# Block-sparse attention with an attention mixture of experts: pairs of heads of the next batch placed between the stages of this one, and one score matmul per query block

## The chip, the cores and the metric

The kernel runs on one core of a Trainium2 chip. The metric is device microseconds (us) for one execution, lower is better. Before the change it took 298.99 us, the median of three runs (298.35 to 299.44).

In what follows, PE is the matrix engine (TensorE; PEld is its loading of weights), DVE the vector engine, ACT the scalar engine, POOL GpSimd, and SP the engine that issues most DMAs. L123 means line 123 of the kernel as it is printed below.

## The reference: what is computed

There are 4 batches, 8 heads, 768 tokens and 64 elements per head. Two layers follow one another.

Layer one is a sparse attention. A query sees the keys at a distance under 16 tokens, and besides them 24 summaries, one for each block of 32 tokens: the summary's key is the elementwise maximum over the block, its value the mean, and log(32) is added to its score. One softmax goes over both kinds.

```
scores_l = where(|i - j| < 16, scale * q @ k.T, -1e9)
scores_s = scale * q @ k_sum.T + log(32)
x = softmax([scores_l, scores_s]) @ [v, v_sum]
```

Layer two takes the heads side by side as x (768 x 512 per batch). A gate picks two of four experts per token with softmaxed weights. Each expert is a causal attention with 64-element queries, keys and values of its own and an output projection back to 512; the output is the weighted sum over the two chosen experts.

## The kernel before

The Tile framework takes the program in the order in which it is written, gives out the buffers and the semaphores, and may move an instruction ahead of others on its engine when its own estimate says that the engine would wait. Each engine then takes its instructions strictly in the order so built; only weight loads of PE run ahead. PSUM (eight banks) is given out from two groups: "one" (one bank, four buffers) and "two" (two banks, two buffers).

The main loop at the end (L336) runs, for each batch, all of `stage1` and then all of `stage2`. Where the next batch's work is independent, the build moves a few of its instructions ahead, no more.

**stage1** (L114) first makes the sums of v by blocks of 32: POOL adds halves of a 96 x 2048 tile, five adds each (L123). Then it goes over four pairs of heads (L128):
- POOL issues the loads of q and k, converting them to 16 bits on the way (L133); 128 consecutive tokens lie across the partitions, six such tiles.
- SP issues the loads of v into `v_blk`, 96 keys on the partitions for each of 12 blocks of 64 queries (L142, L145), and of the block sums into rows 96 to 119 (L148).
- PE transposes q and k (L153, L158), DVE evicts them (L155, L160) and takes the maxima of k over blocks (L162).
- For each head PE writes the mask into the scores by a matmul with the identity (L171), adds the local scores, twelve matmuls of 96 keys by 64 queries with 64 rows contracted (L178), and adds the summaries' scores (L184). Each block's window of 96 keys begins 16 tokens ahead of its queries, but is clamped at both ends (`win_start`).
- ACT takes the exp (L188). PE multiplies with the values in fp32 (L196); column 64 of `v_blk` is a constant and gives the softmax's denominator. DVE divides (L200, L201), PE transposes x (L206), and ACT and DVE split it into two 16-bit parts, hi and lo (L209, L210).

**stage2** (L215) has four parts. *Values and gate*: PE computes the values of the four experts and the gate's logits (L224, L227), DVE copies them (L231, L233) and runs the gate, a dozen operations on 24 elements (L247 to L259). *Two expert parts* (cc = 0 and 1, two experts each): q and k projections (L268), evicted by DVE (L273) and ACT (L275); scores by groups of key tiles (L288), the exp on ACT (L293), the causal cut of the diagonal blocks on POOL (L298), the values (L307), the division and the gate's weight on DVE (L310 to L313), and a transpose (L317, L319). *Output*: the projection (L325), evicted by ACT and DVE (L329, L331), stored by SP (L332).

The weights of stage 2 are loaded after stage 1 of batch 0 is issued (`load_stage2_weights`, L83), through POOL's queue.

Of the kernel before, what the change touches and what calls it, by code (L numbers as in the profile page):

```python
# [8 lines left out]
FP32 = mybir.dt.float32  # L9
# [5 lines left out]
B = 4  # L15
H = 8
S = 768
# [20 lines left out]
def win_start(t):  # L38
    return min(max(64 * t - 16, 0), S - WIN)


@with_exitstack
def kernel(
# [13 lines left out]


# [3 lines left out]
    make_identity(nc, ident32)  # L62

    maskb = consts.tile((128, NQ, 64), HALF, name="maskb")
    nc.gpsimd.memset(maskb, 0.0)
    for t0, t1 in ((0, 1), (1, NQ - 1), (NQ - 1, NQ)):
        shift = 64 * t0 - win_start(t0)
        m = maskb[0:WIN, t0:t1, :]
        n = t1 - t0

        nc.gpsimd.affine_select(m, m, [[0, n], [-1, 64]], AL.is_ge, NEG,
                                base=15 - shift, channel_multiplier=1)
        nc.gpsimd.affine_select(m, m, [[0, n], [1, 64]], AL.is_ge, NEG,
                                base=15 + shift, channel_multiplier=-1)
# [8 lines left out]
    def load_stage2_weights():  # L83
        nc.sync.dma_start(out=wg_f32,
                          in_=moe_w_gate.rearrange("(c p) g -> p c g", p=128))
        for e in range(E):
            cc, ep = divmod(e, 2)
            for j, wsrc in enumerate((moe_wq, moe_wk)):
                nc.gpsimd.dma_start(out=wqk[:, :, cc, j, 64 * ep:64 * ep + 64],
                                    in_=wsrc[e].rearrange("(c p) d -> p c d", p=128))  # L90
            nc.gpsimd.dma_start(out=wvg[:, :, 64 * e:64 * e + 64],
                                in_=moe_wv[e].rearrange("(c p) d -> p c d", p=128))
        for cc in range(2):
            nc.gpsimd.dma_start(out=wo_cat[cc],
                                in_=moe_wo[2 * cc:2 * cc + 2].rearrange("e d n -> (e d) n"))
        nc.vector.tensor_copy(wvg[:, :, 256:260], wg_f32)
        nc.vector.tensor_copy(wg_hi32, wvg[:, :, 256:260])
        nc.vector.tensor_tensor(wg_lo32, wg_f32, wg_hi32, AL.subtract)
        nc.vector.tensor_scalar(wvg[:, :, 260:264], wg_lo32, LO_SCALE, None, AL.mult)


    NVB = 4
    v_bufs = [consts.tile((128, 2, NQ, 65), FP32, name=f"v_blk{i}") for i in range(NVB)]
    for i in range(NVB):
        nc.gpsimd.memset(v_bufs[i][:, :, :, 64:65], 1.0 / XS)
        nc.gpsimd.memset(v_bufs[i][96:128, :, :, 64:65], 32.0 / XS)


    NV2 = 2
    v2_bufs = [consts.tile((128, NT, E, 65), HALF, name=f"v2_{i}") for i in range(NV2)]  # L110
    for i in range(NV2):
        nc.gpsimd.memset(v2_bufs[i][:, :, :, 64:65], XS)

    def stage1(b):  # L114
        xT_hi, xT_lo = [], []
        vsums = []
        for g in range(2):
            v_s = s1.tile((96, 2048), FP32, name="v_s", bufs=2)
            nc.sync.dma_start(out=v_s,
                              in_=v[b, 4 * g:4 * g + 4].rearrange("h (n s) d -> (h n) (s d)", s=32))  # L120
            half = 1024
            while half >= 64:
                nc.gpsimd.tensor_tensor(v_s[:, 0:half], v_s[:, 0:half],  # L123
                                        v_s[:, half:2 * half], AL.add)
                half //= 2
            vsums.append(v_s)

        for c in range(NCH):  # L128
            q_nat = s1.tile((128, NT, 128), HALF, name="q_nat", bufs=3)
            k_nat = s1.tile((128, NT, 128), HALF, name="k_nat", bufs=3)  # L130
            for src, dst in ((q, q_nat), (k, k_nat)):
                for hp in range(2):
                    nc.gpsimd.dma_start(  # L133
                        out=dst[:, :, 64 * hp:64 * hp + 64],
                        in_=src[b, 2 * c + hp].rearrange("(t p) d -> p t d", p=128))
            v_blk = v_bufs[(NCH * b + c) % NVB]
            vb = v[b, 2 * c:2 * c + 2]
            for hp in range(2):
                vh = v[b, 2 * c + hp]
                src = bass.AP(vh.tensor, vh.offset + 48 * D,  # L140
                              [[D, WIN], [64 * D, NQ - 2], [1, D]])
                nc.sync.dma_start(out=v_blk[0:WIN, hp, 1:NQ - 1, 0:64], in_=src)  # L142
                src = bass.AP(vh.tensor, vh.offset,
                              [[D, WIN], [(S - WIN) * D, 2], [1, D]])
                nc.sync.dma_start(out=v_blk[0:WIN, hp, 0:NQ:NQ - 1, 0:64], in_=src)  # L145
                hh = 2 * (c % 2) + hp
                vs = vsums[c // 2][NSUM * hh:NSUM * hh + NSUM, 0:64]
                nc.sync.dma_start(out=v_blk[WIN:KR, hp, :, 0:64],  # L148
                                  in_=vs.unsqueeze(1).to_broadcast((NSUM, NQ, 64)))

            qT_ps = ps.tile((128, NT, 128), HALF, name="qT_ps", tag="one", bufs=4)
            for t in range(NT):
                nc.tensor.transpose(qT_ps[:, t, :], q_nat[:, t, :], ident16)  # L153
            qT = s1.tile((128, S), HALF, name="qT", bufs=2)
            nc.vector.tensor_copy(qT, qT_ps.rearrange("p t n -> p (t n)"))  # L155
            kT_ps = ps.tile((128, NT, 128), HALF, name="kT_ps", tag="one", bufs=4)
            for t in range(NT):
                nc.tensor.transpose(kT_ps[:, t, :], k_nat[:, t, :], ident16)  # L158
            kT = s1.tile((128, S), HALF, name="kT", bufs=2)
            nc.vector.tensor_copy(kT, kT_ps.rearrange("p t n -> p (t n)"))  # L160
            ksum = s1.tile((128, NSUM), HALF, name="ksum", bufs=2)
            nc.vector.tensor_reduce(ksum, kT.rearrange("p (n w) -> p n w", w=32),  # L162
                                    AX.X, AL.max)

            aTs = []
            sps = []
            for hp in range(2):
                sc = ps.tile((128, 1024), FP32, name="sc", tag="two", bufs=2)
                sps.append(sc)
                for lo, hi in ((0, 512), (512, 768)):  # L170
                    nc.tensor.matmul(sc[:, lo:hi], ident16,  # L171
                                     maskb.rearrange("p t n -> p (t n)")[:, lo:hi],
                                     start=True, stop=False, skip_group_check=True)
            for t in range(NQ):
                for hp in range(2):
                    rows = slice(64 * hp, 64 * hp + 64)
                    w0 = win_start(t)
                    nc.tensor.matmul(sps[hp][0:WIN, 64 * t:64 * t + 64],  # L178
                                     kT[rows, w0:w0 + WIN], qT[rows, 64 * t:64 * t + 64],
                                     start=False, stop=False, skip_group_check=True)  # L180
            for hp in range(2):
                rows = slice(64 * hp, 64 * hp + 64)
                for lo, hi in ((0, 512), (512, 768)):
                    nc.tensor.matmul(sps[hp][WIN:KR, lo:hi], ksum[rows, :], qT[rows, lo:hi],  # L184
                                     start=False, stop=True, skip_group_check=True)
            for hp in range(2):
                aT = s1.tile((128, S), FP32, name="aT", bufs=4)
                nc.scalar.activation(aT[0:KR, :], sps[hp][0:KR, 0:S], AF.Exp, scale=SCALE)  # L188
                aTs.append(aT)

            x32 = s1.tile((128, NT, 128), FP32, name="x32", bufs=2)
            for hp in range(2):
                av = ps.tile((128, NT, 65), FP32, name="av", tag="one", bufs=4)
                for t in range(NQ):
                    o = 64 * (t % 2)
                    nc.tensor.matmul(av[o:o + 64, t // 2, :],  # L196
                                     aTs[hp][0:KR, 64 * t:64 * t + 64],
                                     v_blk[0:KR, hp, t, :], start=True, stop=True)
                rec = s1.tile((128, NT, 1), FP32, name="rec", bufs=4)
                nc.vector.reciprocal(rec, av[:, :, 64:65])  # L200
                nc.vector.tensor_tensor(x32[:, :, 64 * hp:64 * hp + 64], av[:, :, 0:64],  # L201
                                        rec.to_broadcast((128, NT, 64)), AL.mult)
# [168 lines left out]
```

The softmax here doesn't subtract the row's maximum and nothing guards it: scores larger than these inputs give would overflow.

## Time and profile before

One execution was profiled. Its time and what it shows in sum:

| | |
|---|---|
| median of the three runs | 298.99 us |
| the profiled execution, its own time | 300.52 us |
| its span, first to last instruction | 298.8 us |
| mean granted TensorE clock | 0.859 of full |
| PE busy / DVE / ACT / POOL | 218.1 / 123.0 / 96.0 / 127.1 us |
| DMA | 32.10 MB in 109001 packets, 104880 of them under 512 bytes |
| POOL's issues of q and k loads (L133) | 64, 53.6 us together |
| PE matmul instructions | 2448 |

The columns of a timeline row are: start and length in us, engine, line, operation, out<-in, how many; in brackets how long the engine had been idle before it and what released it. A row of a table by stretch has the stretch, its length, the busy time of PE, PEld, DVE, ACT and POOL with the number of instructions in parentheses, the granted clock, the share of the DMA engines and GB/s. In the page's slices each digit is the busy share of a fortieth of the span in tenths; for PEclk it is the granted clock.

Busy time says little by itself here: an engine that waits for another half of the time shows as half busy, and the end is set by the chain through several of them.

### The profile page before, as it was taken

Reading aid. Unit: us, or ns where it says so; the run is one execution under the profiler, and the core shown is the slowest. Engines: PE = TensorE matmul, PEld = TensorE weight load, DVE = VectorE, ACT = ScalarE, POOL = GpSimd, SP = SyncE. Lnnn points to the kernel's source line nnn. Section 1 sums busy time; section 2 is a strip of 40 time slices with the busy share of each in tenths; the row PEclk is TensorE's granted clock in tenths of the full one; section 3 lists DMA queues with packets and bytes.
Section 4 is the critical chain, followed back from the end, with each engine's and each line's share of the span. In section 5 each row is a group of like instructions: output and inputs, shape, how many; then the busy total and the mean of one; then the engine's idle time right before and its main releaser. Section 6 shows DMA issues by size and latency. Waiting matters only on the chain.

```text
span 298.8 us, 5906 instructions
## 1 busy us (share of the span) xinstructions
PE 218.1 (73%) x2448; PEld 140.8 (47%) x2448; DVE 123.0 (41%) x280; ACT 96.0 (32%) x117; POOL 127.1 (43%) x191
## 2 busy tenths in 40 slices
PE   1004998492678798877978888697789799679683
PEld 0002766360245466653544666462555566545340
DVE  0002655348042456654407366361425555461231
ACT  1001233205325433316261333307242433225612
POOL 7998543599603444892134249903024000003110
PEclk9999999867587999998675999976867999895957
DMA  7899999993920999939205999993009300000005
GB/s 199 124 81 173 169 168 191 135 119 50 176 49 0 155 232 220 171 79 177 56 0 39 309 225 103 157 184 70 2 0 133 133 2 2 2 0 2 0 0 211
DMA packets 109001, 32.10 MB, mean 107 GB/s; under 512 B 104880, under 2 KB 105136, under 8 KB 108208
## 3 DMA queue, kind: packets, MB, share of 16 engines
q0 software_dynamic: 56800, 7.35, 38.5%
q1 hardware_dynamic: 52176, 24.39, 37.7%
q8 instruction: 19, 0.31, 0.4%
q14 instruction: 6, 0.05, 0.1%
HBM read 30.42 MB, written 6.29 MB: 123 GB/s over the span
## 4 chain that ended last, share of the span: by engine, by line
PE 46%; DVE 22%; ACT 12%; POOL 9%; DMA 5%; issue 4%; SPq 0%; ACTq 0%; POOLq 0%
PE sp L288 7%; PE pp L268 6%; POOL v_s L123 6%; PE av L196 6%; PE av L307 6%; DVE xT_lo L210 5%; ACT a L293 4%; PE op L325 4%; PE sc L178 4%; ACT aT L188 4%; DVE ksum L162 4%; DVE x L201 4%; PE vp L224 3%; PE sc L171 3%; DMA v_s<-in_v_dram 3%
## 5 line engine op out<-in xcount | busy, mean ns | idle before, releaser
L298 POOL TENSOR_SCALAR_AFFINE_SELECT a<-a 128x256 f16<-128x256 f16 x48 | 19.4, 406 | 102.5 <-ACT a L293 102.5
L293 ACT ACTIVATE a<-sp 128x1024 f16<-128x1024 f32 (+1 forms) x48 | 41.2, 921 | 13.4 <-PE sp L288 13.4
L188 ACT ACTIVATE aT<-sc 120x768 f32<-120x768 f32 x32 | 25.5, 810 | 54.3 <-PE sc L184 54.3
L133 POOL DMA_DIRECT2D q_nat<-in_q_dram x32 | 26.9, 850 | 36.8 <-PE qT_ps L153 31.6
L123 POOL TENSOR_TENSOR v_s<-v_s 96x1024 f32<-96x1024 f32 (+4 forms) x40 | 40.6, 1023 | 3.4 <-DMA v_s<-in_v_dram 1.8
L288 PE MATMUL sp<-qkT,qkT 64*128 64x512 f16 (+3 forms) x128 | 27.8, 364 | 19.0 <-ACT a L293 10.4
L196 PE MATMUL av<-v_blk,aT 120*64 120x65 f32 x768 | 29.8, 231 | 5.1 <-ACT aT L188 2.9
L196 PEld LDWEIGHTS av<-v_blk,aT 120*64 120x64 f32 x768 | 25.9, 143 | 12.4 <-ACT aT L188 7.0
L307 PEld LDWEIGHTS <-a 128*128 128x128 f16 x336 | 20.3, 129 | 21.1 <-POOL a L298 17.8
L307 PE MATMUL av<-v,a 128*128 128x65 f16 x336 | 25.5, 242 | 5.1 <-POOL a L298 5.0
L209 ACT CAST xT_hi<-xT_ps 128x768 f16<-128x768 f32 x16 | 12.8, 798 | 47.4 <-PE xT_ps L206 47.4
L310 DVE RECIPROCAL r<-av 128x6 f32<-128x6 f32 x16 | 3.0, 190 | 60.6 <-PE av L307 60.6
L133 POOL DMA_DIRECT2D k_nat<-in_k_dram x32 | 26.7, 854 | 1.5 <-DMA k_nat<-in_k_dram 1.5
L200 DVE RECIPROCAL rec<-av 128x6 f32<-128x6 f32 x32 | 6.3, 196 | 50.5 <-PE av L196 50.5
L268 PE MATMUL pp<-xT_hi,wqk 128*128 128x512 f16 (+1 forms) x128 | 27.0, 358 | 0.0
L178 PEld LDWEIGHTS <-kT 64*96 64x96 f16 x384 | 18.8, 126 | 10.4 <-issue 5.7
L171 PE MATMUL sc<-maskb,ident 128*128 128x512 f16 x64 | 16.1, 337 | 10.3 <-DVE xT_lo L210 5.0
L178 PE MATMUL sc<-qT,kT 64*96 64x64 f16 x384 | 22.3, 212 | 0.6 <-DVE kT L160 0.6
L224 PE MATMUL vp<-wvg,xT_hi 128*128 128x264 f16 x96 | 19.1, 342 | 4.8 <-DMA wvg<-in_moe_wv_dram 3.1
L288 PEld LDWEIGHTS <-qkT 64*128 64x128 f16 x128 | 8.8, 98 | 28.0 <-issue 12.0
L153 PE MATMUL qT_ps<-ident,q_nat 128*128 128x128 f16 x96 | 9.4, 244 | 15.7 <-DMA q_nat<-in_q_dram 15.7
L325 PE MATMUL op<-wo_cat,wT 128*128 128x512 f16 x48 | 19.1, 536 | 1.1 <-DVE wT L319 0.7
(62 smaller groups left out, 272.1 us busy)
## 6 DMA issues: line engine op xcount, KB each, us to landing
v_blk<-in_v_dram SPq DMA_DIRECT2D x32, 240.0 KB
v_s<-in_v_dram SPq DMA_DIRECT2D x8, 768.0 KB
out_dram<-o_sb SPq DMA_DIRECT2D x12, 512.0 KB
q_nat<-in_q_dram POOLq DMA_DIRECT2D x32, 96.0 KB, 5.3
k_nat<-in_k_dram POOLq DMA_DIRECT2D x32, 96.0 KB, 6.5
v_blk<-v_s SPq DMA_DIRECT2D x32, 72.0 KB
v_blk<-in_v_dram SPq DMA_DIRECT2D x32, 48.0 KB
wqk<-in_moe_wq_dram POOLq DMA_DIRECT2D x4, 64.0 KB, 13.3
```

The lines of the kernel that those rows point to most:

```text
L123: nc.gpsimd.tensor_tensor(v_s[:, 0:half], v_s[:, 0:half], v_s[:, half:2 * half], AL.add)
L133: nc.gpsimd.dma_start(out=dst[:, :, 64 * hp:64 * hp + 64], in_=src[b, 2 * c + hp].rearrange("(t p) d -> p t d", p=128))
L171: nc.tensor.matmul(sc[:, lo:hi], ident16, maskb.rearrange("p t n -> p (t n)")[:, lo:hi], start=True, stop=False, skip_group_check=True)
L178: nc.tensor.matmul(sps[hp][0:WIN, 64 * t:64 * t + 64], kT[rows, w0:w0 + WIN], qT[rows, 64 * t:64 * t + 64], start=False, stop=False, skip_ ...
L188: nc.scalar.activation(aT[0:KR, :], sps[hp][0:KR, 0:S], AF.Exp, scale=SCALE)
L196: nc.tensor.matmul(av[o:o + 64, t // 2, :], aTs[hp][0:KR, 64 * t:64 * t + 64], v_blk[0:KR, hp, t, :], start=True, stop=True)
L224: nc.tensor.matmul(vp[:, i, 0:264], xT_hi[ch][:, cols], wvg[:, ch, :], start=(ch == 0), stop=False, skip_group_check=True)
L268: nc.tensor.matmul(pp[:, lo:hi], wqk[:, ch, cc, j, :], xT_hi[ch][:, lo:hi], start=(ch == 0), stop=(ch == NCH - 1))
L288: nc.tensor.matmul(sp[:, c0:c0 + w], kT[rows, 128 * tj:128 * tj + 128], qT[rows, n0:n0 + w], start=True, stop=True)
L293: nc.scalar.activation(a2s[ep][:, base:base + ln], sp[:, 0:ln], AF.Exp, scale=SCALE / (XS * XS))
L307: nc.tensor.matmul(av2[:, ti, :], a2s[ep][:, o:o + 128], v2[:, tj, e, :], start=(tj == 0), stop=(tj == ti))
L325: nc.tensor.matmul(op[:, i, :], wavT[cc][:, 2 * t2 + i, :], wo_cat[cc], start=(cc == 0), stop=(cc == 1))
```

## The change

- **Scores.** For each head and pair there are two persistent tiles. `QB` has the head's 64 query rows, and an identity in the other 64 rows. `KB` has, for each of 12 blocks, 128 columns: 96 keys of the window and 24 block maxima in the head's own 64 rows, and in the other 64 rows the mask. One matmul per block with 128 rows contracted gives the local scores, the mask and the summaries' scores at once. There are two sets (`NB`), used in turn. DVE copies keys, maxima and queries into them.
- **Circular ranges.** Every window begins 16 tokens ahead of its block and wraps round at the ends; kT is 800 wide with 16 columns copied to each end. `v_blk` has 13 blocks: DMAs fill 64 rows, and DVE copies the first 32 rows of block t+1 to rows 64 to 95 of block t.
- **q and k.** SP loads them in fp32, six consecutive tokens on a partition; POOL converts and permutes them; ACT evicts their transposes with a stride of six.
- **Order.** `stage1` becomes `stage1_pair(b, c)`. The four pairs of batch 0 come first, with the loads of the stage-2 weights after each. Then each of the four parts of stage 2 of batch b is followed by one pair of batch b+1.
- **Buffers.** PSUM: "one" has two buffers, "two" has three. In the expert parts the two experts' score matmuls alternate.
- **Constants** are mostly set by DVE, and the first q and k loads are issued ahead of them.

Values, gate, projections and output are computed by the same instructions as before. The core of the diff:

```diff
+    def two(name):
+        return ps.tile((128, 1024), FP32, name=name, tag="two", bufs=3)
+
+    def one(shape, dt, name):
+        return ps.tile(shape, dt, name=name, tag="one", bufs=2)
...
+    def load_qk(b, c):
+        tiles = []
+        for src, name in ((k, "k_f"), (q, "q_f")):
+            t = s1.tile((128, 2, NT, 64), FP32, name=name, bufs=3)
+
+            nc.sync.dma_start(
+                out=t.rearrange("p h j d -> p h (j d)"),
+                in_=src[b, 2 * c:2 * c + 2].rearrange("h (p j) d -> p h (j d)", j=NT))
+            tiles.append(t)
+        return tiles
+
+    def narrow_qk(tiles):
+        out16 = []
+        for t, name in zip(tiles, ("k_nat", "q_nat")):
+            n = s1.tile((128, NT, 2, 64), HALF, name=name, bufs=2)
+            nc.gpsimd.tensor_copy(n, t.rearrange("p h j d -> p j h d"))
+            out16.append(n)
+        return out16
...
+            t = consts.tile((128, NQ, 64), HALF, name=f"QB{i}{hp}")
+            nc.vector.tensor_copy(
+                t[oth], ident16[oth, oth].unsqueeze(1).to_broadcast((64, NQ, 64)))
...
+            t = consts.tile((128, NQ, 128), HALF, name=f"KB{i}{hp}")
...
-            for src, dst in ((q, q_nat), (k, k_nat)):
-                for hp in range(2):
-                    nc.gpsimd.dma_start(
-                        out=dst[:, :, 64 * hp:64 * hp + 64],
-                        in_=src[b, 2 * c + hp].rearrange("(t p) d -> p t d", p=128))
...
-                for lo, hi in ((0, 512), (512, 768)):
-                    nc.tensor.matmul(sc[:, lo:hi], ident16,
-                                     maskb.rearrange("p t n -> p (t n)")[:, lo:hi],
-                                     start=True, stop=False, skip_group_check=True)
...
+    def stage1_pair(b, c):
+        st = state.setdefault(b, {"hi": [], "lo": [], "vs": {}})
+        k_nat, q_nat = narrow_qk(qk_first if (b, c) == (0, 0) else load_qk(b, c))
+        v_blk = load_v(b, c)
+        if c % 2 == 0:
+            st["vs"][c // 2] = load_vsum(b, c // 2)
+            sum_v(st["vs"][c // 2])
+        for hp in range(2):
+            hh = 2 * (c % 2) + hp
+            vs = st["vs"][c // 2][NSUM * hh:NSUM * hh + NSUM, 0:64]
+            nc.sync.dma_start(out=v_blk[WIN:KR, hp, 0:NQ, 0:64],
+                              in_=vs.unsqueeze(1).to_broadcast((NSUM, NQ, 64)))
+            nc.vector.tensor_copy(v_blk[64:96, hp, 0:NQ, :], v_blk[0:32, hp, 1:NQ + 1, :])
+
+        qb, kb = QB[c % NB], KB[c % NB]
+        kT_ps = one((128, NT, 128), HALF, "kT_ps")
+        for j in range(NT):
+            nc.tensor.transpose(kT_ps[:, j, :], k_nat[:, j].rearrange("p h d -> p (h d)"), ident16)
+        kT = s1.tile((128, 800), HALF, name="kT", bufs=2)
+        nc.scalar.copy(kT[:, 16:784].rearrange("c (p j) -> c p j", j=NT),
+                       kT_ps.rearrange("c j p -> c p j"))
+        nc.vector.tensor_copy(kT[:, 0:16], kT[:, 768:784])
+        nc.vector.tensor_copy(kT[:, 784:800], kT[:, 16:32])
...
+        nc.scalar.copy(qT.rearrange("c (p j) -> c p j", j=NT),
+                       qT_ps.rearrange("c j p -> c p j"))
...
+        for hp in range(2):
+            own = slice(64 * hp, 64 * hp + 64)
+            kw = kT[own, :]
+            nc.vector.tensor_copy(
+                kb[hp][own, :, 0:WIN],
+                bass.AP(kw.tensor, kw.offset, [list(kw.ap[0]), [64, NQ], [1, WIN]]))
+            nc.vector.tensor_copy(kb[hp][own, :, WIN:KR],
+                                  ksum[own].to_broadcast((64, NQ, NSUM)))
+            nc.vector.tensor_copy(qb[hp][own].rearrange("p t n -> p (t n)"), qT[own])
+
+        aTs = []
+        for hp in range(2):
+            sc = two("sc")
             for t in range(NQ):
...
+                nc.tensor.matmul(sc[:, 64 * t:64 * t + 64], kb[hp][:, t, :], qb[hp][:, t, :],
+                                 start=True, stop=True)
+            aT = s1.tile((128, S), FP32, name="aT", bufs=4)
+            nc.scalar.activation(aT[0:KR, :], sc[0:KR, 0:S], AF.Exp, scale=SCALE)
+            aTs.append(aT)
...
+    for c in range(NCH):
+        stage1_pair(0, c)
+        load_stage2_weights(c)
     for b in range(B):
-        x = stage1(b)
-        if b == 0:
-            load_stage2_weights()
-        stage2(b, *x)
+        parts = (lambda: values_and_gate(b), lambda: experts(b, 0),
+                 lambda: experts(b, 1), lambda: output(b))
+        for c in range(NCH):
+            parts[c]()
+            if b + 1 < B:
+                stage1_pair(b + 1, c)
```

## The prediction

> **What bounds the kernel now.** I read the page's shares and slices first, then the time by stage, then one stage as a timeline.
>
> The page, parts 1 and 2:
>
> ```profile
> PE 218.1 (73%) x2448; PEld 140.8 (47%) x2448; DVE 123.0 (41%) x280; ACT 96.0 (32%) x117; POOL 127.1 (43%) x191
> ...
> PE   1004998492678798877978888697789799679683
> ...
> PEclk9999999867587999998675999976867999895957
> ```
>
> No engine is full over the span, and the granted TensorE clock falls and recovers four times, once per batch. Cut at the stages of batches 1 and 2 (stretch; length; busy times; clock):
>
> ```profile
> 130.00:165.80 35.80, 29.84 (x243) 17.44 (x243) 15.11 (x41) 14.09 (x17) 12.86 (x21) 0.76 0.48 87
> 165.80:193.50 27.70, 23.15 (x372) 16.99 (x371) 14.30 (x28) 9.41 (x12) 19.04 (x21) 1.00 1.25 190
> 193.50:230.70 37.20, 31.04 (x242) 17.97 (x243) 15.11 (x41) 14.32 (x18) 9.16 (x18) 0.72 0.57 77
> ```
>
> Stage 1 (27.7 us, four pairs of heads, 7.17 us each) keeps PE busy 83% at full clock. Stage 2 (35.8 to 37.2 us) is PE and ACT in turn, at 0.72 to 0.76. A batch is 64.8 us. The first expert part of batch 2:
>
> ```profile
> 202.46 0.62 PE L288 MATMUL sp<-qkT,qkT 64*128 64x512 f16 x6 [0.89 <-ACT qkT L275]
> ...
> 206.26 1.62 ACT L293 ACTIVATE a<-sp 128x1024 f16<-128x1024 f32 x2 [0.16 <-PE sp L288]
> ...
> 208.83 0.41 POOL L298 TENSOR_SCALAR_AFFINE_SELECT a<-a 128x256 f16<-128x256 f16 x1 [0.48 <-ACT a L293]
> ...
> 208.95 1.97 PE L307 MATMUL av<-v,a 128*128 128x65 f16 x32
> ...
> 210.72 1.97 PE L268 MATMUL pp<-xT_hi,wqk 128*128 128x512 f16 x9
> ...
> 212.53 0.50 PE L317 MATMUL wT_ps<-ident,wav 128*128 128x128 f16 x6
> ```
>
> Six exps on ACT set its pace (5.5 us). Only 11 of the next part's 16 projections (L268) fill PE's gaps. So the kernel is bound by chains through PE, ACT and DVE; taking work from PE pays only where PE is what comes last.
>
> **What the change takes and adds.** The built order of the changed kernel gives the counts.
>
> PE: per pair it removes four mask matmuls (216 ns start to start), four summary matmuls (222) and 24 score matmuls of 96 weight columns (45): some 2.7 us. It adds 24 with 128x128 weights and 64 columns. Nearest is L307 (128x128 weights, 65 columns): 39 ns at full clock, 55 at half, so 0.9 to 1.3 us. That is -1.6 us x 16 = -26 us of PE busy time. If PE alone bound the kernel, this would be the gain.
>
> ACT takes over the k and q evictions: 2 x 0.80 us a pair (768 columns cost 796 to 810 ns at L275, L209, L188); DVE gives up 2 x 0.55 (L155, L160).
>
> DVE gets, per pair, ten copies between SBUF tiles, which no row shows. Floor: a small DVE operation, 0.17 us. Ceiling: the rates of copies out of PSUM (768 f16 in 0.55; 768 f32 in 0.96). So key window (1152 f16) 0.17 to 0.75, sums (288) 0.17 to 0.31, queries (768) 0.17 to 0.55, v rows (780 f32) 0.17 to 0.98. The ends are far apart and neither row is nearer; I take the middles: 0.46, 0.24, 0.36, 0.57. One pair's two heads: 2.1 us (1.0 to 3.2), and 1.1 for v.
>
> POOL loses 64 descriptor-writing issues of 0.85 us (-54) and gets 32 narrowing copies of 768 elements; L65 sets as many in 0.74, and a two-input add of 1024 takes 2.33 (L123), so 0.75 to 1.8, taken 1.15: +37. All loads now stand in SP's queue, eleven issues of 0.4 to 1.4 us a pair, behind waits for the sums on POOL. They are issued a pair or more ahead, and pairs come every 18 us, so I cost them at nothing; without that cover one late load would hold the narrowing and then the pair, some 3 us. Fewer, longer packets only help: DMA is no bound, at a share of 0.5 to 1.4 of its engines. The two heads of the expert scores now alternate and the two-bank buffers are three, not two; ACT's exps (back to back today but for 0.2 us gaps) cover that, so it is worth under 0.5 us a part.
>
> **Where it lands.** The order is the point. PE takes instructions in order, and in the built program a pair of the next batch stands whole *between* two parts of stage 2: after the first expert part's last transposes come k and q transposes, both heads' scores, both heads' values, the x transposes, and only then the next projections. Nothing of stage 2 stands inside the pair, and with two one-bank buffers instead of four k's transposes cannot move ahead. The projections that filled gaps (L268 above) now stand behind the pair too. So the stages alternate rather than overlap, and I add them up.
>
> A pair behind an expert part, full clock / half clock: k transposes to eviction 0.55/0.88; ACT 0.80; two edge copies 0.42; key maxima 0.95 (L162); copies for two heads 2.12; last scores 0.57/0.76; exp 0.88 with its latency; values of one head 0.97/1.43 (24 records at 38.9 and 29.5 us); reciprocal and scaling 0.86; x transposes 0.68/1.3. Sum 8.8/10.4, taken 9.6. Today L178 starts right after the eviction, with the maxima beside it; now maxima and copies stand ahead of the first score. That wait replaces what the masks cost.
>
> Expert part, alone: projections and ACT eviction 3.65 (198.81 to 202.46), scores to last transpose 9.7 (5.5 exps, 0.7 before, 3.5 after; today 10.4 and 9.6): 13.4, with projections at half clock 15.8; taken 13.9.
>
> Values, gate and pair 0: scores of pair 0 follow the whole of the value matmuls; 11.0/13.3, taken 12.3. Output and pair 3: q's eviction stands behind two ACT output copies (1.01 each): 10.2/14, taken 12. Pair 2 carries pair 3's k transposes, +0.5.
>
> A batch: 12.3 + 13.9 + 9.6 + 13.9 + 10.1 + 12 = 71.8, against 64.8.
>
> Start: the first values wait for the v sums; POOL has eight weight issues (0.74) and four narrowings ahead of or between those adds, so they end near 24.5 (17.9 today); DVE's some thirty constant copies and memsets, at most 0.6 each, are done by 17 and hidden behind that. Values run from 27 to 29.9 (to 32.4 today). The next three pairs take 9.1 each, not 7.17: the chain above to the second head's values (7.2/8.2), plus xT_lo 0.96 and, in two of three, one v copy 0.57, which stand in DVE's queue ahead of the scores (8.6/9.6). Then 1.9 to the last x transposes: 59.1 (56.2 today).
>
> End: the last stage 2 has no partner and keeps its hoisted projections: 41.2, as from 257.6 to 298.8 today.
>
> **Port contention** comes on top. The same operation beside POOL's adds and with POOL idle:
>
> ```profile
> 71.93 2.22 DVE L259 TENSOR_TENSOR g_b<-wu,rg 128x24 f32<-128x24 f32 x1
> ```
>
> ```profile
> 202.85 0.18 DVE L259 TENSOR_TENSOR g_b<-wu,rg 128x24 f32<-128x24 f32 x1
> ```
>
> Batch 0's gate chain took 6.9 us for 1.85. Those operations read two SBUF tiles. The maxima (one SBUF input) at 185.6 us took 953 ns beside an add, as alone. The new copies have one input too, but write as much as they read; they lie between the rows. By the first row, in POOL's order the adds and narrowings run beside pair 1's copies (+3.4) and a little of the others': 4.8 a batch, 3 in the first stage; by the second, nothing. I take half: 2.4 and 1.5. The Trainium skill, GPSIMD Engine Reference, section 8, says that POOL shares its SBUF interfaces with VectorE and contends with instructions in a two-port mode. By it the full price stands and the sum is 9 us higher; it speaks against moving work into SBUF copies.
>
> **Sum.** 59.1 + 1.5 + 3 x (71.8 + 2.4) + 41.2 = 324.4 us span. The profiled run lay 1.7 above its span (300.52 and 298.8) and 1.5 above the median (298.99), so the forecast is **324.6 us**, some 9% slower.
>
> **Rivals.**
>
> *The clock stays full* (faster). Every part at its full-clock price: 11.0 + 13.4 + 8.8 + 13.4 + 9.3 + 10.2 = 66.1; first stage 56.2 (28.9 + 3 x 8.6 + 1.5); the last stage 2 some 36, as its 28.8 busy us at clock 0.72 hold 8 that a full clock would save, of which I count 5; 291 with no contention. It decides where the interleaved batch falls under (298.8 - 59.1 - 41.2)/3 = 66.2, which needs a granted clock over some 0.95 there. For: pairs put 4 us of PE work into each gap. Against: in batch 2 the clock fell at 204.5, after 3.5 us with PE busy about half (1.11 and 0.84 of 2 us), and a pair is busy about 45%. The Trainium skill, TensorE: Matmul & The Clock Gate, Part 1, has half clock follow a whole idle window of some 3.4 us; by it the longest new gap (eviction to scores, 4 us) would mostly pass and the sum would be nearer 300. The row decides for me.
>
> *DVE becomes the bound* (slower still). Copies at PSUM rates (+1.1 x 16 pairs = 18) or contention in full (+9): 333 with the one, 342 with the other, 351 with both.
>
> *The interleaving does more than the order shows*: only if waits of one stage ended early, PE's order being fixed; it would show as no change.
>
> **How the numbers follow.** Forecast 0.62 (308 to 337); DVE bound 0.22 (337 to 352); clock 0.12 (285 to 297.5); no change 0.04. About 0.3% (0.9 us) can be told from no change. Leaving out the clock case and the upper edge gives 302 to 350. Faster 0.12, same 0.04, slower 0.84. The extremes of all prices (285 and 372) are left out as they need every price at one end.
>
> **What would show it.** Right: in the interleaved batches PE idle 3 to 4 us between q transposes and scores, released by DVE's copies; pairs of 9 to 11 us; clock near 0.7; POOL idle more. Wrong: copies of the key window under 0.25 us, pair chains under 8 us, a batch under 66, a clock near 1.0; or the start ending before 55 us. If SP's queue is what narrowing waits for, my zero there is wrong.

## The result and the profile after

The changed kernel takes **339.17 us**, the median of four runs (337.48 to 342.84), against 298.67 us for the kernel before (four runs, 297.46 to 299.44). The ratio is 1.134, with a 95% interval of 1.128 to 1.141: slower by 40.5 us, where 25.6 were forecast. The direction and the range hold; the size is 14.6 us short. Medians here and below are of all runs, while ratios and intervals leave out the runs in a slower state (here the one of 342.84), so the two can differ a little.

The profiled execution took 337.48 us, its span is 335.7. The page's first two parts (busy time and instructions of each engine; then busy tenths in forty slices):

```profile
PE 199.7 (59%) x2320; PEld 149.8 (45%) x2320; DVE 182.2 (54%) x445; ACT 119.3 (36%) x149; POOL 100.1 (30%) x144
...
PE   1025644838628636687638648744746766677871
...
DVE  2996568485174175687275076495245414744321
...
PEclk9999767876757855899757858795765675999879
```

PE lost 18 us of busy time and yet is at 59% in place of 73%: it waits more. The clock now lies at 0.5 to 0.8 for most of the span; before, it recovered in every stage 1. DVE is busy for 59 us more than before. Cut at the last x transposes of each batch (stretch; length; busy times of PE, PEld, DVE, ACT and POOL; clock; DMA share; GB/s), the three batches in which pairs stand between the parts of stage 2 are:

```profile
63.20:145.64 82.44, 50.92 (x588) 38.86 (x587) 45.06 (x105) 30.35 (x38) 27.27 (x36) 0.71 0.45 112
145.64:217.30 71.66, 47.80 (x583) 36.10 (x581) 39.89 (x102) 29.64 (x37) 15.94 (x24) 0.76 0.44 103
217.30:298.44 81.14, 51.00 (x577) 37.83 (x575) 41.75 (x100) 28.73 (x36) 20.03 (x28) 0.71 0.33 84
```

The first stage ends at 63.2, and the last stage 2 takes 37.3. Before, the first stage ended at 56.1, the three batches took 73.0, 63.7 and 64.8, and the last stage 2 took 41.2. So the loss is 7 us at the start and 9, 8 and 16 in the batches, less 4 at the end. The two long batches are the two in which POOL is busiest, and that is the lead. Here is the pair behind the second expert part of batch 0, as a timeline:

```profile
120.69 0.85 PE L217 MATMUL kT_ps<-ident,k_nat 128*128 128x128 f16 x6
...
122.44 0.81 DVE L221 COPY kT<-kT 128x16 f16<-128x16 f16 x1 [0.96 <-ACT kT L219]
123.17 0.16 DVE L222 COPY kT<-kT 128x16 f16<-128x16 f16 x1
123.20 5.88 POOL L194 TENSOR_TENSOR v_s<-v_s 96x1024 f32<-96x1024 f32 x5
123.24 0.94 DVE L230 TENSOR_REDUCE ksum<-kT 128x24 f16<-128x768 f16 x1
124.10 1.75 DVE L236 COPY KB<-kT 64x1152 f16<-64x1152 f16 x1
125.77 1.28 DVE L239 COPY KB<-ksum 64x288 f16<-64x288 f16 x1
126.98 0.34 DVE L241 COPY QB<-qT 64x768 f16<-64x768 f16 x1
...
127.38 0.80 PE L247 MATMUL sc<-QB,KB 128*128 128x64 f16 x12 [5.04 <-DVE QB L241]
```

PE finishes the transposes of q and then stands for 5.04 us, until DVE has filled the operands of the first score matmul. The same copies take 0.46 (L236) and 0.23 us (L239) elsewhere in this trace, without POOL beside them. A narrow window around one of them shows why they take 1.75 and 1.28 here:

```profile
124.10 1.75 DVE L236 COPY KB<-kT 64x1152 f16<-64x1152 f16 x1
125.61 1.35 POOL L194 TENSOR_TENSOR v_s<-v_s 96x512 f32<-96x512 f32 x1
125.77 1.28 DVE L239 COPY KB<-ksum 64x288 f16<-64x288 f16 x1
```

POOL's first add runs from 123.20 to 125.53; the window copy begins inside it and ends 0.3 us after it. The next add runs to 126.97; the copy of the sums begins inside that one and ends 0.1 us after it. In this stretch DVE and POOL take turns, a whole instruction at a time.

### The profile page after: what moved, and what is told of

It reads as the page before. It is cut to its first block, busy times and chain, and to the rows that moved or that the text cites. A ratio compares the mean times of both kernels' runs of the same rounds, so it can differ in the third digit from the quotient of the medians.

```text
span 335.7 us, 5871 instructions
## 1 busy us (share of the span) xinstructions
PE 199.7 (59%) x2320; PEld 149.8 (45%) x2320; DVE 182.2 (54%) x445; ACT 119.3 (36%) x149; POOL 100.1 (30%) x144
## 4 chain that ended last, share of the span: by engine, by line
PE 24%; DVE 18%; ACT 12%; issue 8%; POOL 1%; ACTq 0%; DVEq 0%; POOLq 0%
PE av L258 5%; ACT a L364 5%; PE pp L337 5%; PE op L398 3%; PE xT_ps L268 2%; ACT aT L250 2%; PE av L377 2%; PE sc L247 2%; DVE ksum L230 2%; ACT kT L219 2%; DVE wav L383 2%; DVE x L263 2%; DVE cmb L382 2%; DVE v_blk L212 1%; DVE KB L236 1%
## 5 line engine op out<-in xcount | busy, mean ns | idle before, releaser
L247 PE MATMUL sc<-QB,KB 128*128 128x64 f16 x384 | 23.6, 232 | 64.7 <-DVE QB L241 64.0
L247 PEld LDWEIGHTS <-KB 128*128 128x128 f16 x384 | 21.5, 122 | 67.4 <-DVE KB L239 46.2
L258 PE MATMUL av<-v_blk,aT 120*64 120x65 f32 x768 | 42.4, 298 | 7.7 <-issue 3.9
L258 PEld LDWEIGHTS av<-v_blk,aT 120*64 120x64 f32 x768 | 39.4, 209 | 10.2 <-ACT aT L250 5.7
L219 ACT COPY kT<-kT_ps 128x768 f16<-128x768 f16 x16 | 12.8, 799 | 62.9 <-PE kT_ps L217 50.1
L77 POOL CAST k_nat<-k_f 128x768 f16<-128x768 f32 x16 | 13.4, 838 | 48.6 <-PE kT_ps L217 31.6
L337 PE MATMUL pp<-xT_hi,wqk 128*128 128x512 f16 (+1 forms) x128 | 26.7, 366 | 0.1
L272 DVE TENSOR_TENSOR xT_lo<-xT_ps,xT_hi 128x768 f16<-128x768 f32 x16 | 15.2, 951 | 14.7 <-ACT xT_hi L271 14.7
L212 DVE COPY v_blk<-v_blk 32x780 f32<-32x780 f32 x32 | 18.9, 597 | 7.2 <-DMA v_blk<-in_v_dram 6.1
L268 PE MATMUL xT_ps<-ident,x 128*128 128x128 f32 x96 | 16.5, 317 | 10.0 <-DVE x L263 9.8
L263 DVE TENSOR_TENSOR x<-av,rec 128x384 f32<-128x384 f32 x32 | 17.8, 558 | 1.1
```

The source lines that it names most:

```text
L212: nc.vector.tensor_copy(v_blk[64:96, hp, 0:NQ, :], v_blk[0:32, hp, 1:NQ + 1, :])
L219: nc.scalar.copy(kT[:, 16:784].rearrange("c (p j) -> c p j", j=NT), kT_ps.rearrange("c j p -> c p j"))
L247: nc.tensor.matmul(sc[:, 64 * t:64 * t + 64], kb[hp][:, t, :], qb[hp][:, t, :], start=True, stop=True)
L258: nc.tensor.matmul(av[o:o + 64, t // 2, :], aTs[hp][0:KR, 64 * t:64 * t + 64], v_blk[0:KR, hp, t, :], start=True, stop=True)
L268: nc.tensor.transpose(xT_ps[:, 128 * t:128 * t + 128], x32[:, t, :], ident32)
L337: nc.tensor.matmul(pp[:, lo:hi], wqk[:, ch, cc, j, :], xT_hi[ch][:, lo:hi], start=(ch == 0), stop=(ch == NCH - 1))
```

## Experiments

Theory: two costs of about the same size, which add. (1) **Order**: a pair stands whole between two parts of stage 2, so its chain of eviction, maxima and copies is waited for, and the projections that filled gaps are gone. (2) **Adds**: DVE's new copies wait for POOL's instructions, and POOL's narrowings stand behind its adds. Rivals: the order hides something and the new pair alone is dear; the order alone is the loss; late sums, not the adds themselves; the smaller group of one-bank buffers.

Times below are medians of four runs, with the ratio to the kernel before on the same chip and its 95% interval.

**1. The changed kernel in the old order.**

```diff
-            parts[c]()
-            if b + 1 < B:
-                stage1_pair(b + 1, c)
+            stage1_pair(b, c)
...
+        values_and_gate(b)
+        experts(b, 0)
+        experts(b, 1)
+        output(b)
```

> The changed kernel with all its new pairs, copies and buffers, but in the old order: four pairs of a batch, then the whole of its stage 2. Main theory (in the built order a pair stands whole between two parts of stage 2, so the stages alternate and the order hides nothing, while it takes away the projections that used to fill gaps): faster than the changed kernel; 63 for the first stage, three further stages 1 of about 35 to 38 (pairs behind one another overlap a little, the POOL adds come early) and stages 2 of 37 each: 316 to 328 us. Rival 1 (interleaving does hide part of a pair, and the loss sits in the new pair's own copies and waits): 340 us or more. Rival 2 (the order alone is the whole loss, the new pair is no dearer than the old one of 7.2 us): 300 us or less.

Measured: 317.03 us, 1.059 (1.052 to 1.065). The order costs 22 us of the 40; the rest is in the pairs.

**2. The kernel before in the new order.**

```diff
-        x = stage1(b)
-        stage2(b, *x)
+        parts = stage2(b)
+        for c in range(NCH):
+            next(parts, None)
+            if b + 1 < B:
+                stage1(b + 1, [c])
```

> The kernel before, with its own scores, loads and buffers; only the order is changed: a pair of the next batch follows each of the four parts of stage 2. Main theory (the order costs the hoisted projections and brings the clock down, about half of the 40 us that the changed kernel lost): 308 to 320 us. Rival 1 (the new pair's copies and their waits are the whole loss): 295 to 302 us. Rival 2 (interleaving hides work when the pairs are cheap on DVE): under 293 us.

Measured: 310.19 us, 1.037 (1.030 to 1.043). With the old pair, whose scores start right after the eviction, the same order costs 11.0 us (299.17 for the kernel before on that chip), half as much. In this order PE's granted clock is 0.78, 0.90 and 0.90 in the three batches (0.71, 0.76, 0.71 with the new pairs).

**3. The changed kernel without POOL's adds.**

```diff
-            sum_v(st["vs"][c // 2])
+            pass
```

> The changed kernel without POOL's adds: the block sums of v are left out, and the first row of each block stands in their place. Nothing else changes. If DVE's copies lose time beside POOL's adds at the full price (the gate's and the pairs' operations that take 3 to 5 times as long there) and the values wait for the late sums: 15 to 25 us faster than the changed kernel, 314 to 324 us. If alternation and the chain of copies carry the loss, and contention only the half price of the forecast plus the waits at the start: 5 to 12 us faster, 327 to 334 us. If neither, 337 to 340 us.

Measured: 315.51 us, 1.052 (1.043 to 1.061). The adds are worth 24 us. The same stretches as above:

```profile
59.10:134.50 75.40, 52.17 (x588) 39.68 (x587) 38.71 (x105) 30.32 (x38) 10.49 (x19) 0.72 0.41 105
134.50:205.90 71.40, 48.51 (x582) 36.29 (x581) 38.56 (x100) 29.62 (x37) 11.98 (x20) 0.76 0.44 118
205.90:278.40 72.50, 49.06 (x576) 37.03 (x575) 38.19 (x100) 28.82 (x36) 9.94 (x18) 0.74 0.35 94
```

The middle batch is as long as with the adds (71.4 and 71.7), the outer two lose 7 and 9 us. DVE has the same instructions but 6.4, 1.3 and 3.6 us less busy time: it had been charged with waiting. The clock is nearly the same, so it is not what made those batches long.

What PE waited for divides the difference (engine, line, releaser: us in total, times, longest), first with the adds, then without:

```profile
PE sc L247 <- DVE QB L241: 64.0, 18, 16.0
PE wT_ps L387 <- DVE wav L383: 16.6, 8, 3.3
PE kT_ps L217 <- POOL k_nat L77: 5.0, 1, 5.0
PE av L258 <- issue: 3.9, 2, 3.2
```

```profile
PE sc L247 <- DVE QB L241: 54.1, 18, 11.1
PE wT_ps L387 <- DVE wav L383: 10.2, 8, 1.7
PE kT_ps L217 <- POOL k_nat L77: 5.0, 1, 5.0
```

The scores' operands account for 9.9 us, of which 4.9 lie ahead of the very first score (16.0 and 11.1). Another 6.4 lie in the expert parts, ahead of the transposes of `wav`: there the product L382, an instruction that the kernel before has too (L312), takes 0.17 us alone and up to 1.58 beside an add, and two v copies take 1.01 in place of 0.56. Another 3.9, put down to "issue" (nothing that the profile shows), are values whose rows of the sums were stored only just before. That is 20.2 in all, where the spans differ by 19.6; the rest of the list differs little, both ways. For a narrowing PE waits once, 5.0 us, with the adds and without them: the narrowings that stand behind adds are not what PE waits for in this kernel.

**4. The old order and no adds.** Both edits together.

> The changed kernel in the old order (317.0 us) and without POOL's adds; the block sums of v are left out. With the changed kernel, the one without adds and the one in the old order it makes a square of order by adds. If both effects are apart: 317 less 24, 290 to 297 us. If the adds hurt only where pairs stand between parts of stage 2: 310 to 317 us. If the new pair without adds were no dearer than the old pair: 285 us or less.

Measured: 295.56 us, 0.989 (0.982 to 0.996). The square of order by adds is:

| | with adds | without |
|---|---|---|
| pairs between the parts | 339.2 | 315.5 |
| stages in sequence | 317.0 | 295.6 |

Rows differ by 22.1 and 20.0, columns by 23.7 and 21.5: over the whole span the two effects add, and neither needs the other. Batch by batch they do not: in the three batches of the profiled runs the order costs 11.6, 0.3 and 9.3 us with the adds and 10.1, 4.4 and 4.1 without. (The kernel before, 298.7, has the adds too. What it would gain without them was not run, so the lower right corner is no verdict on the new pair.)

**5. Adds on a scratch tile** (inconclusive). The sum is taken of a tile that nothing else touches.

```diff
-            sum_v(st["vs"][c // 2])
+            sum_v(scratch)
```

> The changed kernel with POOL's adds of the block sums done at the same place and in the same number, but on a scratch tile that nothing waits for; the block sums of v themselves are left out, as in the run without adds (315.5 us against 339). It parts the 24 us that the adds cost into two. Theory A (DVE's copies lose time beside POOL's adds, wherever the result goes): 330 to 340 us. Theory B (what costs is that the values, and the loads behind them in SP's queue, wait for sums that come late): 314 to 320 us. Both about half: 322 to 330.

Measured: 345.14 us, 1.162 (1.152 to 1.171), more than either theory expected. POOL's timeline shows why:

```profile
26.50 34.15 POOL L194 TENSOR_TENSOR scratch<-scratch 96x256 f32<-96x256 f32 x30
60.59 0.82 POOL L77 CAST k_nat<-k_f 128x768 f16<-128x768 f32 x1
```

With nothing to wait for, the build moved thirty adds in front of the third pair's narrowing: the first stage ends at 85.0, and the batches, now free of adds, take 75.9, 71.1 and 72.4, as in run 3. It does not separate the wait for the sums from the adds themselves, but it shows that the adds cost where they stand, and that thirty of them ahead of a narrowing hold its pair.

**6. Adds tied to their load, result unread.**

```diff
-            nc.gpsimd.tensor_tensor(v_s[:, 0:half], v_s[:, 0:half],
-                                    v_s[:, half:2 * half], AL.add)
+        t = s1.tile((96, 1024), FP32, name="unread", bufs=2)
+        nc.gpsimd.tensor_tensor(t, v_s[:, 0:1024], v_s[:, 1024:2048], AL.add)
...
+            nc.gpsimd.tensor_tensor(t[:, 0:half], t[:, 0:half], t[:, half:2 * half], AL.add)
```

> The changed kernel with POOL's forty adds in their old places, tied to the load of their source by the first add, but their result goes to a tile that nothing reads; the block sums of v are left out of the output. It mends the earlier run on a scratch tile, in which the build stacked thirty adds into the first stage, so that it told nothing of the batches. Theory A (the adds cost by DVE's copies and POOL's narrowings that stand beside or behind them): 332 to 340 us, as with the sums read. Theory B (the values and SP's queue wait for late sums): 315 to 321 us, as without adds.

Measured: 339.62 us, 1.135 (1.127 to 1.144), the same as with the sums read. So late sums are not the main cost; the adds cost mainly by standing beside DVE's instructions. The subtraction is not exact, for the adds moved: the three batches take 79.4, 77.9 and 78.4, with POOL busy 16.8, 22.0 and 20.1 us, in place of 82.4, 71.7 and 81.1 with 27.3, 15.9 and 20.0. The 3.9 us of late values in the changed kernel may be hidden in that. In the trace of the changed kernel, DVE instructions that overlap POOL and take longer than the median of their kind (kinds of eight or more) exceed it by 16.2 us in sum, 10.8 beside adds and 5.4 beside narrowings; 4.4 of it is the product L382, not a new copy.

**7. The old buffers.** Four one-bank and two two-bank buffers.

```diff
-        return ps.tile((128, 1024), FP32, name=name, tag="two", bufs=3)
+        return ps.tile((128, 1024), FP32, name=name, tag="two", bufs=2)
...
-        return ps.tile(shape, dt, name=name, tag="one", bufs=2)
+        return ps.tile(shape, dt, name=name, tag="one", bufs=4)
```

> The changed kernel with PSUM given out as before the change: four one-bank buffers and two of two banks, in place of two and three. Main theory (the order of the program sets where a pair stands; more one-bank buffers let some of k's transposes move ahead, while scores, values and copies stay behind the part of stage 2): 334 to 342 us. Rival (the two one-bank buffers are what keeps the pair whole, as a sentence of the forecast has it): 325 us or less.

Measured: 340.91 us, 1.142 (1.134 to 1.151): no difference that can be told. The one-bank buffers are not what keeps a pair whole: the rival's 15 us are not there. (The same edit takes a two-bank buffer away, and the last stage 2 is 2.5 us longer, 39.8 in place of 37.3, so a gain of that size may be hidden.)

**8. Each pair prepared ahead.** If the chain is what PE waits for, it has to start earlier: `stage1_pair` is cut after the copies.

```diff
-    def stage1_pair(b, c):
+    def prepare(b, c):
...
+    def attend(b, c):
...
         for c in range(NCH):
+            if b + 1 < B:
+                prepare(b + 1, c)
             parts[c]()
             if b + 1 < B:
-                stage1_pair(b + 1, c)
+                attend(b + 1, c)
```

> The changed kernel with each pair cut in two: loads, transposes, evictions and the copies into the score operands are written ahead of the part of stage 2 that goes before the pair, and scores, values and x transposes after it. In the built order the scores then stand inside the part. Main theory (the chain of eviction, maxima and copies, some 5 us a pair, is what PE waits for): the chain is hidden beside the part, 12 pairs x 3 to 5 us less, so 280 to 305 us. Rival (DVE's time and POOL's adds are the bound, whatever the order): 325 us or more, since the same copies then delay the part's own DVE operations.

Measured: 307.19 us, 1.026 (1.020 to 1.033): 32 us faster than the changed kernel, at the same DVE busy time (182.5), which the rival excluded. It misses the forecast of 280 to 305, and the view of waits has a new entry (engine, line, releaser: us in total, times, longest):

```profile
PE av L262 <- DMA v_blk<-v_s: 21.6, 3, 10.4
```

The rows of the sums come late, because their source is loaded late in SP's queue, behind stores that wait.

**9. Prepared ahead, loads a pair earlier.**

```diff
-        k_nat, q_nat = narrow_qk(qk_first if (b, c) == (0, 0) else load_qk(b, c))
-        v_blk = load_v(b, c)
+        if i + 1 < NCH * B:
+            loads(i + 1)
+        qk, v_blk, vsrc = loaded.pop(i)
+        k_nat, q_nat = narrow_qk(qk)
```

> The version with each pair prepared ahead, with POOL's adds kept, and every load (the source of the sums too) issued a pair earlier in SP's queue, ahead of the store into the value tiles that waits for the sums. There PE had waited 21.6 us for rows of the sums that came by a late load. If the late load is the cause: 284 to 294 us. If the adds themselves and their contention are: 302 to 308 us.

Measured: 289.47 us, 282.39 to 290.75. The lowest of the four runs lies 7 us below the others, so no interval is given; the profile is of the run of 289.56. All four lie at least 15 us below run 8, and the wait for the rows of the sums falls from 21.6 us to 4.4. Late loads were the cause (the edit moves all loads of a pair, not the sums' source alone).

**10. As 9, with the sums by PE in place of POOL.** Six fp32 matmuls a pair with a 0/1 matrix, and loads a pair earlier as well.

```diff
-            sum_v(st["vs"][c // 2])
+            nc.tensor.matmul(vs_ps, ind[:, j, :], v_n[:, :, j, :],
+                             start=(j == 0), stop=(j == NT - 1))
```

> The version with each pair prepared ahead (307.2 us), and in it the block sums of v by six fp32 matmuls a pair with a 0/1 matrix in place of POOL's forty adds; loads are issued a pair ahead. If the adds and their late results cost there what they cost in the changed kernel (24 us), less some 1 us a pair of new PE work: 278 to 292 us, faster than the kernel before. If DVE's own work (60% busy) is the bound: 298 to 306 us.

Measured: 288.86 us, 0.969 (0.964 to 0.973). It is within the expectation, but the reason given for it falls: run 9 keeps the adds and is as fast to within what can be told. (Run 10 has 22.6 us of new PE work, so a small gain may hide behind it; 24 us do not.) The line of busy times on the page of run 9, and of run 10:

```profile
PE 185.6 (65%) x2320; PEld 137.1 (48%) x2320; DVE 185.5 (65%) x445; ACT 117.9 (41%) x149; POOL 102.4 (36%) x144
```

```profile
PE 208.2 (73%) x2512; PEld 162.1 (56%) x2512; DVE 165.9 (58%) x463; ACT 118.0 (41%) x149; POOL 59.2 (21%) x106
```

DVE's copies still wait for POOL in run 9 (DVE is 20 us busier than in run 10), but they stand ahead of a part of stage 2 and PE has other work: a stretched copy costs only where PE waits for it.

**11. The kernel before, prepared ahead.** Old scores, old loads, old adds; the cut of run 8 on the order of run 2.

```diff
+            ready[b] = (qT, kT, ksum, v_blk)
+
+    def attend(b, c):
...
+            if b + 1 < B:
+                prepare(b + 1, [c])
             next(parts, None)
             if b + 1 < B:
-                stage1(b + 1, [c])
+                attend(b + 1, c)
```

> The kernel before, with its old scores, loads, buffers and adds, in the interleaved order (310.2 us), but with each pair's loads, transposes, evictions and maxima written ahead of the part of stage 2 and its scores and values after it. If what the interleaved order lacks is only that a pair's chain starts early, and the new score operands are worth little even then: 285 to 296 us. If the gain of the prepared versions of the changed kernel comes from the cheaper scores on PE (some 1.6 us a pair): 303 to 311 us.

Measured: 294.01 us, 0.987 (0.979 to 0.994): 16 us less than run 2 by the early chain alone, and 1.3% less than the kernel before. Its page has 25 us more PE work than that of run 9:

```profile
PE 210.9 (72%) x2448; PEld 137.5 (47%) x2448; DVE 123.3 (42%) x280; ACT 95.0 (32%) x117; POOL 127.2 (44%) x191
```

With the new scores, loads and buffers the same order took 289.5 (run 9; its lowest run 282.4). So with all else prepared, the whole change, with its 25 us less of PE time, is worth 5 us by the medians and 12 by run 9's lowest run. In the profiled runs the three batches give 6.7 and the last stage 2, where no pair is left, 3.4 (41.4 here, 38.0 in run 9), while the first stage is 5.3 longer (64.0 in place of 58.7). What the one-matmul scores are worth by themselves was not separated from the loads and buffers.

**12. As 10, the first stage prepared ahead too.**

```diff
+    prepare(0, 0)
     for c in range(NCH):
-        prepare(0, c)
+        if c + 1 < NCH:
+            prepare(0, c + 1)
         attend(0, c)
```

> The prepared version with the sums on PE (288.9 us), and each pair prepared before the scores of the pair ahead of it in the first stage too, where the pairs took 11 us each against 7.2 before the change; later batches are prepared as there. Theory (a pair's chain of evictions and copies is what the first stage waits for): 2 to 4 us a pair in three pairs, 278 to 284 us. Rival (DVE, busy with the pair's own copies, is the bound there): 287 to 290 us.

Measured: **280.45 us** (277.02 to 283.31), 0.930 (0.922 to 0.938), the fastest version and 6 to 7% faster than the kernel before. The first stage ends at 50.4 (61.5 in run 10), and the batches and the last stage 2 are together as long as there (224.8 and 225.5). Its second expert part of batch 0, PE alone:

```profile
92.56 0.64 PE L270 MATMUL sc<-QB,KB 128*128 128x64 f16 x9
93.04 0.35 PE L400 MATMUL av<-v,a 128*128 128x65 f16 x3
93.20 0.83 PE L270 MATMUL sc<-QB,KB 128*128 128x64 f16 x12
93.84 1.95 PE L400 MATMUL av<-v,a 128*128 128x65 f16 x32
95.60 0.35 PE L270 MATMUL sc<-QB,KB 128*128 128x64 f16 x3
96.89 0.82 PE L410 MATMUL wT_ps<-ident,wav 128*128 128x128 f16 x6 [0.94 <-DVE wav L406]
```

The scores (L270) of the next batch's pair now lie among the values (L400) of this batch's expert part, in PE's gaps. In the changed kernel they all stood behind it.

## Why the prediction was right and where it was wrong

- **Strict order of PE, pairs whole between parts, stages that alternate**: right. Run 1 prices the order at 22 us, and starting the chain a part earlier (run 8) gives back 32.
- **The sum without contention**: 315.7 forecast, 316.1 the span of run 3, where the adds are absent. That this is so close is luck, for errors cancel: the three batches are 3.9 longer (215.4 forecast, 219.3 measured) and the last stage 2 is 3.5 shorter. Within the batches, by pairs' ends and in the sum of three: values, gate and pair 0 36.9 forecast and 43.2 measured; first expert part and pair 70.5 and 74.0; second 72.0 and 69.9; output and pair 36.0 and 32.2.
- **Port contention at half price**: this is the step that failed. "I take half: 2.4 and 1.5" makes 8.7 us over the span. The spans with and without adds differ by 19.6 (335.7 and 316.1), the medians by 23.7. The row that was to argue for half, key maxima unharmed beside an add, was read rightly (0.95 us beside and alone in the changed kernel too), but a reduction is not a copy. The Trainium skill, SBUF — State Buffer, section "SBUF: two separate sides", says that DVE and POOL share one pair of ports by an exclusive lock held for a whole instruction, which DVE needs with two SBUF inputs or in a two-port mode. The timeline above agrees, with 1.75 us in place of 0.46. At the full price that the forecast worked out, the sum would have been 333. What the forecast left out of that price, by the waits under run 3: the constants' copies at the start, the product L382 and the late values. They are not an exact account of the 6 us that remain.
- **Prices of the copies**: right, all four. Alone they take 0.46, 0.23, 0.355 and 0.557 us; taken were 0.46, 0.24, 0.36 and 0.57. No row stood behind the middles that were taken, so that is luck. The narrowing takes 0.82 (taken 1.15).
- **26 us of PE busy time**: 18 measured. The price is right (25 us between runs 11 and 9; the terms taken away add up to 2.8 a pair and not 2.7). But at the lower clock other work got longer: the same 768 value matmuls take 42.4 us (L258) in place of 29.8 (L196).
- **Values, gate and pair 0 at 12.3**: too low, 17.1, 10.7 and 18.3 measured (17.0, 12.9 and 13.3 without the adds). The forecast let the pair's chain begin behind the value matmuls and forgot DVE's own queue there. Before the first score of the next batch, in order on DVE:

```profile
69.77 0.56 DVE L212 COPY v_blk<-v_blk 32x780 f32<-32x780 f32 x1
70.36 0.18 DVE L314 SCALAR_TENSOR_TENSOR lg<-lgp 128x24 f32<-128x24 f32 x1
70.58 0.56 DVE L212 COPY v_blk<-v_blk 32x780 f32<-32x780 f32 x1
71.17 0.18 DVE L316 TENSOR_REDUCE m<-lg 128x6 f32<-128x24 f32 x1
71.26 0.44 DVE L236 COPY KB<-kT 64x1152 f16<-64x1152 f16 x1
...
72.45 0.82 PE L247 MATMUL sc<-QB,KB 128*128 128x64 f16 x12 [4.98 <-DVE QB L241]
```

  k and q had been transposed 7 us earlier, but the value copies and the gate's operations stand between. PE waits 4.98 us.
- **Start**: 60.6 with contention forecast, 63.2 measured; 59.1 without the adds, as the forecast's sum without them says. Again two errors cancel. The first pair ends at 30.7 and, without the adds, at 26.7 (31.8 forecast); the next three take 32.5 and 32.4 (27.3 forecast). DVE's constants, "at most 0.6 each" and "done by 17", end at 20.2, and the first score waits for them, not the values for the sums, which are done at 20.2 too (24.5 forecast). Two of the copies wait out POOL, the second one two adds and two narrowings in a row (0.17 alone in run 3):

```profile
12.08 2.43 DVE L118 COPY KB<-mk 64x96 f16<-64x96 f16 x1
...
14.75 3.96 DVE L121 COPY KB<-mk 64x96 f16<-64x96 f16 x1
```

- **Last stage 2 at 41.2**: it takes 37.3. Alternating scores and a third two-bank buffer were costed at "under 0.5 us a part"; every version that has both takes 37.1 to 38.2 there, the three that have neither 41.2 to 41.6, and the changed kernel with two such buffers 39.8 (run 7). The step was mis-sized by 4 us, in the kernel's favour.
- **Loads in SP's queue at nothing, one late load 3 us**: the price is right in the changed kernel (the values of pair 0 of the last batch stand 3.16 us behind late sums, though run 6, in which the adds moved, is no faster without that wait). Once the rest of the chain was hidden, the same queue cost 21.6 us (run 8).
- **Two one-bank buffers keep k's transposes back**: as a cause, wrong (run 7).
- **Rivals**: the clock did not stay full (0.71 to 0.76, some 0.7 was expected), so the row of the trace was the better guide here than the rule that was weighed against it. In the changed kernel the clock also falls where PE was not idle: below, PE is busy for 2.29 of 3.40 us at full clock, with no pause over 0.9 us since 109.0, and then the clock is at half.

```profile
112.40:115.80 3.40, 2.29 (x17) 1.03 (x16) 0.00 (x0) 3.40 (x5) 1.69 (x5) 1.00 0.95 224
115.80:119.20 3.40, 1.99 (x34) 1.78 (x32) 1.56 (x5) 0.45 (x1) 0.73 (x2) 0.50 0.05 12
```

  "DVE becomes the bound" has 333 for contention in full and 342 for copies at PSUM rates (the forecast names them in the other order). 342 is nearer to the result, but its reason is not what happened, for with POOL idle the copies cost the middles. The name is wrong too: DVE is idle 46% of the time, and run 8 at the same DVE busy time is 32 us faster. DVE sets the end only where PE waits for it.

## What to carry to other kernels

Writing two stages' parts in turn does not overlap them when engines take instructions in order: cut the second stage at its long chain, and put the chain (loads, evictions, copies) a part ahead of the matmuls that need it. Work taken from PE is worth nothing while PE waits; here 25 us of it bought nothing as it stood, and once the chains were hidden the whole change was worth 5 to 12. Before moving work to copies between SBUF tiles on DVE, look at what POOL does at that time, and price each copy at the POOL instruction that it may have to wait out.

## What the hardware showed that was not expected

- A copy on DVE with one SBUF input that begins beside a POOL add or narrowing waits out the whole instruction: 16 elements a partition (L221) take 0.17 us alone and up to 0.88 beside POOL, 288 elements 0.23 and up to 1.28. It can lose more than one turn: 96 elements took 3.96 us, over four POOL instructions (L121 at 14.75). Copies out of PSUM (L296, 0.41), reductions (L230, 0.95) and products with one PSUM input (L263, 0.56) take the same time beside POOL as alone.
- A product of two SBUF tiles is held in the same way: six elements a partition (L382) take 0.17 us alone and up to 1.58 beside an add.
- POOL's narrowing, with one input, holds DVE too: 5.4 of the 16.2 us.
- The build moves work with no dependence as far ahead as it can (thirty adds, 34 us), so an experiment that cuts a dependence may also move the work.
